# Half-row output stores: the first right-hand tile by itself, two left-hand tiles in one store, and the evictions around them on other engines

## The chip, the cores and the metric

The kernel runs on one core of a Trainium2 chip. The metric is device time in microseconds (us) of one execution, from its start to its end; lower is better.

## The reference

Pooled attention over eight batches and eight heads feeds a soft mixture of experts. What the change touches is the end of the second part.

```python
# attention: k and v are averaged over 8 neighbours, then softmax(q k^T / 8) v
x = attn_out.transpose(0, 2, 1, 3).reshape(4608, 512)     # one row per token
logits = x @ phi                                          # 4608 x 32 slots
d = softmax(logits, axis=0);  slot_input = d.T @ x        # 32 x 512
for e in range(8):                                        # 4 slots for each expert
    slot_out[e] = relu(slot_input[e] @ w1[e]) @ w2[e]     # 512 -> 1024 -> 512
c = softmax(logits, axis=1)
out = c @ slot_out                                        # 4608 x 512, float32
```

## The kernel before, in words

The first 120 us are attention, in four pairs of batches, with the transposed exponentials of the logits left in `cT` (slots on the partitions, tokens in the free dimension). Meanwhile GpSimd's queue loads `w1` and `w2` from memory, converted to bf16 on the way. Then come the hidden layer (`hidden`, `turn_hidden`), the second layer (`second_layer`, L582), which accumulates the 32 slot outputs in the bank `so_ps`, and the combination of the slots into the tokens.

The output is made in 36 tiles of 128 tokens by 512 columns. A group of `rows` tiles holds `128 * rows` neighbouring tokens, partition p having `rows` of them, so that a whole group is stored with long contiguous runs; `GROUPS` and `TILES` say which tile is row r of which group. `tokens(n)` picks the columns of `cT` for tile n, with a step of `rows // 2`.

The columns are cut into a left and a right half of 256. The weights of the last two experts are loaded half by half (L530, in the pieces `PIECES`), first all pieces of the left half, then those of the right. As soon as a half is complete, `begin` makes its first four tiles: `so_a` is the slot outputs without the very last piece of the weights (J7), whose share comes in by a product with `zT` (L659), so that these tiles need not wait for `so`, which is made behind them from the complete `so_ps`. `put` evicts a tile from PSUM and divides it by the token's sum `recR`; its third argument picks the engine, 0 for ScalarE (L616) and 1 for VectorE (L618). `tiles` makes two further tiles of a half (product L639) and stores them. Tiles 0 to 9 are made and stored in halves; the 26 behind them (groups of 4, 8 and 14 rows) in whole rows, with one store for a group.

All stores are issued by SyncE (SP) at L634 in program order, each waiting for the evictions of its tiles. SP does nothing else. The order of instructions on TensorE, ScalarE, VectorE and SP in this part is the order of the code.

The sums over the slots of each token come from products with a one-hot matrix, chunk by chunk (`chunk_sums`, L429): the first three chunks early, the other seven later in two portions. `quads` and `rest` set the order of the chunks; they are built from `GROUPS`.

Of the kernel before, what the change touches and what calls it, by code (L numbers as in the profile page):

```python
# [18 lines left out]
def kernel(  # L19
# [10 lines left out]
    nc = tc.nc  # L30
# [5 lines left out]
    E = moe_w1.shape[0]  # L36
# [12 lines left out]
    FJ = F // 128  # L49
# [4 lines left out]


    GROUPS, base = [], 0
    for rows in (2, 2, 2, 4, 4, 8, 14):
        GROUPS.append((rows, base))
        base += 128 * rows
    TILES = [(g, r) for g, (rows, _) in enumerate(GROUPS) for r in range(rows)]  # L60
# [13 lines left out]
    cT = persist.tile([128, 2, B * S // 2], BF)  # L74
# [89 lines left out]
    with tc.tile_pool(name="tmp", bufs=1) as tmp:  # L164
# [8 lines left out]
        for r in range(2):  # L173
            rows = slice(r * D, (r + 1) * D)
# [11 lines left out]
        for r in range(2):  # L186
            rows = slice(r * D, (r + 1) * D)
# [219 lines left out]
    for g, (rows, base) in enumerate(GROUPS):  # L407
        cols = cT[:, :, base // 2:base // 2 + 64 * rows].rearrange("p r (i s) -> p s r i", s=rows // 2)
# [44 lines left out]
        nc.vector.reciprocal(out=recR[:, 2:4, 0:len(quads)], in_=ps[:, 2:4, 0:len(quads)])  # L453
        yield

    def tokens(n):

        g, r = TILES[n]
        rows, base = GROUPS[g]
        step, c0 = rows // 2, base // 2 + r // 2  # L460
        return cT[:, r % 2, c0:c0 + 127 * step + 1:step]

    def step(gen):
        if gen is not None:
# [52 lines left out]
    def half_home(e, half):  # L517
        if e == E - 1:
            flat = xsa[:, 1, half * FJ * HC:(half + 1) * FJ * HC]
        else:  # L520
            c0 = CUT6 * DM + half * (FJ - CUT6) * HC
            flat = xsa[:, 0, c0:c0 + (FJ - CUT6) * HC]
        return flat.rearrange("p (j c) -> p j c", c=HC)

    w2_half = {}
    for half, cols in enumerate(halves):
        for e, j0, j1 in PIECES:
            home = half_home(e, half)
# [19 lines left out]
    recC = post.tile([128, 1], FP)  # L548
# [25 lines left out]
    so_ps = ps_o.tile([128, DM], FP, name="so_ps")  # L574

    def second_layer(e, j0=0, j1=FJ, half=None, by=1):

        cols = slice(0, DM) if half is None else halves[half]
        for fj in range(j0, j1):
            g = fj % NG  # L580
            rhs = w2_at[e, fj] if half is None else w2_half[e, fj, half]
            nc.tensor.matmul(out=so_ps[g * NS:(g + 1) * NS, cols].rearrange("p (c s) -> p s c", s=by), lhsT=hT[:, e, fj],  # L582
                             rhs=rhs.rearrange("p (c s) -> p s c", s=by),
                             start=(e == 0 and fj < NG), stop=(e == E - 1 and fj >= NG), skip_group_check=True)
# [12 lines left out]
    J7 = FJ - 1  # L597
# [3 lines left out]
    CARRY = 4  # L601
    z_ps = ps_f.tile([128, 2, 128 * CARRY // 2], FP, name="z_ps", tag="f")
    nc.tensor.matmul(out=z_ps, lhsT=hz, rhs=cT[:, :, 0:128 * CARRY // 2], start=True, stop=True)
    zT = post.tile([128, 2, 128 * CARRY // 2], BF)
# [9 lines left out]
    def scaled(engine, dst, src, by):  # L614
        if engine == 0:
            nc.scalar.activation(out=dst, in_=src, func=AF.Copy, scale=by)  # L616
        else:
            nc.vector.tensor_scalar(out=dst, in0=src, scalar1=by, scalar2=None, op0=ALU.mult)  # L618

    so_a = post.tile([128, DM], BF)  # L620
    so = post.tile([128, DM], BF)

    out_a = exf.rearrange("p (n c) -> p n c", c=DM)
    out_b = w1f.rearrange("p (n c) -> p n c", c=DM)
    n = 0
    places = []
    for rows, base in GROUPS:
        home = out_a[:, n:n + rows] if n + rows <= 6 else out_b[:, n - 6:n - 6 + rows]
        places.append((home, out[base:base + 128 * rows].rearrange("(p r) c -> p r c", r=rows)))
        n += rows  # L630

    def store(g, r0, r1, cols):
        home, dst = places[g]
        nc.sync.dma_start(out=dst[:, r0:r1, cols], in_=home[:, r0:r1, cols])  # L634

    def product(n, cols):
        bank = ps_f.tile([128, DM], FP, name="f_ps", tag="f")
        rhs, times = so[:, cols], 2 if cols == halves[0] and n >= CARRY else 1
        nc.tensor.matmul(out=bank[:, 0:times * (cols.stop - cols.start)].rearrange("p (a c) -> p a c", a=times), lhsT=tokens(n),  # L639
                         rhs=rhs.rearrange("p c -> p () c").to_broadcast([128, times, cols.stop - cols.start]),  # L640
                         start=True, stop=True)
        return bank[:, 0:cols.stop - cols.start]

    def rec(n):
        i, c = place[n]
        return recR[:, i, c:c + 1]

    def put(n, cols, engine, ps):
        g, r = TILES[n]
        scaled(engine, places[g][0][:, r, cols], ps, rec(n))  # L650

    def begin(half, stores):

        cols = halves[half]
        scaled(0, so_a[:, cols], so_ps[:, cols], recC)
        f = []
        for n in range(CARRY):
            f.append(ps_f.tile([128, DM], FP, name="f_ps", tag="f")[:, 0:HC])
            nc.tensor.matmul(out=f[n], lhsT=zT[:, n % 2, n // 2 * 128:n // 2 * 128 + 128], rhs=w2_half[E - 1, J7, half],  # L659
                             start=True, stop=False)  # L660
        for n in range(CARRY):
            nc.tensor.matmul(out=f[n], lhsT=tokens(n), rhs=so_a[:, cols], start=False, stop=True)
        second_layer(E - 1, J7, FJ, half)
        put(0, cols, 0, f[0])
        put(1, cols, 1, f[1])
        put(2, cols, 0, f[2])
        scaled(1, so[:, cols], so_ps[:, cols], recC)
        put(3, cols, 0, f[3])
        for g, r0, r1 in stores:
            store(g, r0, r1, cols)  # L670

    def tiles(n0, n1, half):

        cols = halves[half]
        for n in range(n0, n1):
            put(n, cols, 1 - n % 2, product(n, cols))
        g, r = TILES[n0]
        store(g, r, r + n1 - n0, cols)

# [13 lines left out]
    second_layer(*PIECES[1], 0)  # L693
    busy(192)
    second_layer(*PIECES[2], 0)
    begin(0, ((0, 0, 1), (0, 1, 2), (1, 0, 1), (1, 1, 2)))
    for n in (4, 6):
        tiles(n, n + 2, 0)
    for e, j0, j1 in PIECES[:2]:
        second_layer(e, j0, j1, 1)  # L700
    tiles(8, 10, 0)
    for e, j0, j1 in PIECES[2:-1]:
        second_layer(e, j0, j1, 1)
    begin(1, ((0, 0, 2), (1, 0, 2)))
    for n in (4, 6, 8):
        tiles(n, n + 2, 1)
    for n in range(10, len(TILES)):
        g, r = TILES[n]
# [33 lines left out]
```

## Time and profile before

| | us |
|---|---|
| median of 3 runs | 174.5 (174.48 to 174.53) |
| the profiled execution | 174.42 |
| its span, first to last instruction | 172.6 |

| engine | busy us | share of the span |
|---|---|---|
| TensorE | 131.7 | 76% |
| VectorE | 100.8 | 58% |
| ScalarE | 88.0 | 51% |
| GpSimd | 27.5 | 16% |

The 16 transfer engines moved 41.13 MB, at a mean of 238 GB/s. 30.48 MB of it are loads from GpSimd's queue and 10.49 MB transfers from SP's, of which the output is 9.44 MB. The page gives the busy share of the transfer engines as a row of 40 digits, tenths of each slice of the span (4.3 us). The busy shares of the engines are averages over stages with quite different limits, so the tail of the kernel, from about 144 us, has to be read by itself. The times of a store are its issue on SP (start and duration), the first packets, and its landing. A transfer's duration in the table of DMA issues is from issue to landing, and so includes what it waited behind other transfers.

### The profile page before, as it was taken

How to read it: one execution, taken by the hardware profiler on the slowest of the kernel's cores; microseconds unless marked ns; L12 is line 12 of the kernel's file. 1: busy time of each engine (PE TensorE's matmuls, PEld its weight loads, DVE VectorE, ACT ScalarE, POOL GpSimd, SP SyncE). 2: the span in 40 equal slices, each digit the busy share in tenths (PEclk: the TensorE clock that was granted, in tenths of full speed). 3: DMA queues.
4: the chain of work that ended last, by engine and by line, in shares of the span. 5: the costliest groups of instructions: out<-in, count | busy, mean ns of one | idle time of the engine just before them, and what ended most of it. 6: DMA issues, size and time to landing. Idle time of an engine off the chain costs nothing.

```text
span 172.6 us, 2869 instructions
## 1 busy us (share of the span) xinstructions
PE 131.7 (76%) x1106; PEld 71.1 (41%) x1106; DVE 100.8 (58%) x265; ACT 88.0 (51%) x168; POOL 27.5 (16%) x42
## 2 busy tenths in 40 slices
PE   0005798899999999899789999896899997899000
PEld 0002373556555656556345554452452234433000
DVE  6686152569678667887994858841551103599300
ACT  3201336988496846988601998566021003699100
POOL 7000102020201013205100470130610030000000
PEclk9999999999999999999999999999999999999955
DMA  5999999999999999999999999999999999999994
GB/s 196 244 220 222 209 220 218 209 219 218 209 218 217 216 219 214 216 217 211 218 216 215 216 216 220 216 213 216 216 215 216 208 193 195 321 354 425 490 425 213
DMA packets 10589, 41.13 MB, mean 238 GB/s; under 512 B 704, under 2 KB 6592, under 8 KB 6864
## 3 DMA queue, kind: packets, MB, share of 16 engines
q0 software_dynamic: 7248, 30.48, 87.0%
q1 hardware_dynamic: 3328, 10.49, 15.5%
q8 instruction: 8, 0.13, 0.3%
q14 instruction: 5, 0.04, 0.1%
HBM read 61.93 MB, written 9.44 MB: 413 GB/s over the span
## 4 chain that ended last, share of the span: by engine, by line
PE 34%; DMA 27%; ACT 14%; DVE 13%; issue 3%; POOL 1%; DVEq 0%; ACTq 0%; POOLq 0%
DMA xsa<-in_moe_w_dram 21%; PE pool_ps L232 10%; ACT exa L311 7%; DMA phi_f<-in_moe_phi_dram 7%; DVE xsa L342 6%; PE u_ps L331 5%; PE q_ps L264 5%; PE sc L309 5%; PE G_ps L366 3%; PE turn_ps L248 2%; DVE w_sb L618 2%; ACT vmeans L238 2%; PE f_ps L639 2%; ACT vp L296 2%; ACT w_sb L616 1%
## 5 line engine op out<-in xcount | busy, mean ns | idle before, releaser
L311 ACT ACTIVATE exa<-sc 72x576 bf16<-72x576 f32 x64 | 39.3, 653 | 4.6 <-PE sc L309 3.8
L342 DVE TENSOR_TENSOR xsa<-u_ps,rec 128x384 bf16<-128x384 f32 x69 | 37.8, 554 | 1.7
L331 PE MATMUL u_ps<-vp,exa 128*128 128x97 bf16 (+5 forms) x320 | 31.4, 229 | 3.6 <-DVE xsa L342 3.0
L331 PEld LDWEIGHTS <-exa 128*128 128x128 bf16 (+1 forms) x320 | 18.9, 100 | 15.7 <-DVE xsa L342 6.4
L309 PE MATMUL sc<-qTa,kp 64*72 64x288 bf16 x128 | 20.6, 303 | 1.7 <-ACT exa L311 1.2
L232 PE MATMUL pool_ps<-big,pmat 128*128 128x512 bf16 x64 | 18.2, 410 | 0.7 <-ACT qTa L268 0.7
L336 DVE RECIPROCAL rec<-u_ps 128x4 f32<-128x4 f32 x72 | 11.9, 174 | 10.8 <-PE u_ps L331 10.5
L268 ACT COPY qTa<-q_ps 128x768 bf16<-128x768 bf16 x8 | 6.4, 794 | 13.1 <-PE q_ps L264 13.1
L184 PE MATMUL phi_ps<-spread,sel 128*128 128x256 bf16 x4 | 1.3, 395 | 15.0 <-DVE spread L179 15.0
L264 PE MATMUL q_ps<-ident,big 128*128 128x128 bf16 x144 | 12.4, 230 | 0.2
L639 PE MATMUL f_ps<-so,cT 128*128 128x512 bf16 (+1 forms) x38 | 10.1, 361 | 2.0 <-DVE so L618 1.3
L240 DVE TENSOR_REDUCE rsum<-rest_ps 128x64 f32<-128x512 f32 x8 | 5.5, 691 | 10.1 <-PE rest_ps L236 10.1
L309 PEld LDWEIGHTS <-kp 64*72 64x72 bf16 x128 | 7.8, 107 | 8.9 <-issue 3.5
L618 DVE TENSOR_SCALAR w_sb<-f_ps,recR 128x512 f32<-128x512 f32 (+1 forms) x17 | 10.5, 679 | 0.6 <-PE f_ps L639 0.5
L264 PEld LDWEIGHTS <-big 128*128 128x128 bf16 x144 | 9.6, 103 | 2.5 <-issue 1.0
L270 DVE COPY qTa<-q_ps 128x768 bf16<-128x768 bf16 x16 | 8.7, 551 | 2.6 <-PE q_ps L264 2.6
L616 ACT ACTIVATE w_sb<-f_ps,recR 128x512 f32<-128x512 f32 (+1 forms) x17 | 9.5, 637 | 0.7 <-PE f_ps L639 0.5
L530 POOL DMA_DIRECT2D xsa<-in_moe_w_dram x8 | 5.9, 743 | 22.3 <-DMA qTa<-in_moe_w_dram 8.9
L366 PE MATMUL G_ps<-xsa,ee 128*128 128x512 bf16 x36 | 8.4, 379 | 1.2 <-ACT ee L361 1.2
L232 PEld LDWEIGHTS <-pmat 128*128 128x128 bf16 x64 | 6.0, 102 | 6.9 <-issue 2.4
L238 ACT CAST vmeans<-pool_ps 128x1024 bf16<-128x1024 f32 x4 | 4.0, 1012 | 6.8 <-PE pool_ps L232 6.8
L616 ACT ACTIVATE so_a<-so_ps,recC 128x256 bf16<-128x256 f32 x2 | 0.9, 470 | 12.4 <-PE so_ps L582 12.4
(109 smaller groups left out, 168.8 us busy)
## 6 DMA issues: line engine op xcount, KB each, us to landing
w_sb<-in_moe_w_dram POOLq DMA_DIRECT2D x2, 3072.0 KB, 36.7
big<-in_q_dram POOLq DMA_DIRECT2D x4, 1152.0 KB, 12.5
big<-in_v_dram POOLq DMA_DIRECT2D x4, 1152.0 KB, 15.8
big<-in_moe_w_dram POOLq DMA_DIRECT2D x1, 4096.0 KB, 33.3
out_dram<-w_sb SPq DMA_DIRECT2D x1, 3584.0 KB, 10.6
big<-in_k_dram POOLq DMA_DIRECT2D x3, 1152.0 KB, 21.3
w_sb<-in_moe_w_dram POOLq DMA_DIRECT2D x2, 1024.0 KB, 18.3
qTa<-in_moe_w_dram POOLq DMA_DIRECT2D x1, 2048.0 KB, 30.1
```

The source lines that it names most:

```text
L232: nc.tensor.matmul(out=ps, lhsT=pmat, rhs=src[:, t:full * POOL:POOL, :], start=(t == 0), stop=(t == POOL - 1))
L264: nc.tensor.transpose(out=ps[:, t].rearrange("p n i -> p (n i)"), in_=q_sb[pair][:, tt:tt + 2, :].rearrange("p t d -> p (t d)"), identity= ...
L270: nc.vector.tensor_copy(out=dst, in_=ps)
L309: nc.tensor.matmul(out=ps[:, r, 0:S // 2], lhsT=kp[pair][rows, n], rhs=qT[pair][rows, n].rearrange("p t i -> p (t i)"), start=True, stop=True)
L311: nc.scalar.activation(out=dst.rearrange("p r (i t) -> p r i t", t=NU), in_=ps[:, :, 0:S // 2].rearrange("p r (t i) -> p r i t", i=NI), fu ...
L331: nc.tensor.matmul(out=bank[rows, hh * UW:(hh + times) * UW].rearrange("p (a c) -> p a c", a=times), lhsT=ex[b][:, hh].rearrange("p r t -> ...
L336: nc.vector.reciprocal(out=rec, in_=ps[:, :, XW])
L342: nc.vector.tensor_tensor(out=dst, in0=ps[:, :, 0:XW], in1=rec.rearrange("p h -> p h ()").to_broadcast([128, HQ, XW]), op=ALU.mult)
L366: nc.tensor.matmul(out=ps, lhsT=ee[:, t].rearrange("p g s -> p (g s)"), rhs=x[:, t, :, 0:D], start=(t == 0), stop=(t == 8))
L616: nc.scalar.activation(out=dst, in_=src, func=AF.Copy, scale=by)
L618: nc.vector.tensor_scalar(out=dst, in0=src, scalar1=by, scalar2=None, op0=ALU.mult)
L639: nc.tensor.matmul(out=bank[:, 0:times * (cols.stop - cols.start)].rearrange("p (a c) -> p a c", a=times), lhsT=tokens(n), rhs=rhs.rearran ...
```

## The change

There are four edits.

1. The groups of the tiles that are made in halves are of 4 and 6 rows, where they were of 2, 2, 2 and 4; the groups of 4, 8 and 14 rows behind them stay. Tiles keep their numbers, but hold other tokens.
2. The right half stores tile 0 by itself, then tiles 1 and 2, then tile 3; before, it stored tiles 0 and 1, then 2 and 3.
3. The left half stores tiles 0 and 1 by themselves as before, and tiles 2 and 3 in one store instead of two.
4. In the left half, tiles 0, 1 and 2 go to ScalarE and tile 3 to VectorE, with `so` ahead of all of VectorE's evictions; the piece of the second layer that `so` needs stands behind the first of the four products instead of the last. In `tiles`, the even tile of the left half goes to ScalarE and the odd one to VectorE, the other way round from before. In the right half the order and the engines stay.

The core of the diff:

```diff
-    for rows in (2, 2, 2, 4, 4, 8, 14):
+    for rows in (4, 6, 4, 8, 14):
...
         for n in range(CARRY):
             nc.tensor.matmul(out=f[n], lhsT=tokens(n), rhs=so_a[:, cols], start=False, stop=True)
-        second_layer(E - 1, J7, FJ, half)
+            if n == (0 if half == 0 else CARRY - 1):
+                second_layer(E - 1, J7, FJ, half)
         put(0, cols, 0, f[0])
-        put(1, cols, 1, f[1])
-        put(2, cols, 0, f[2])
-        scaled(1, so[:, cols], so_ps[:, cols], recC)
-        put(3, cols, 0, f[3])
-        for g, r0, r1 in stores:
-            store(g, r0, r1, cols)
+        if half == 0:
+            scaled(1, so[:, cols], so_ps[:, cols], recC)
+            put(1, cols, 0, f[1])
+            put(2, cols, 0, f[2])
+            put(3, cols, 1, f[3])
+        else:
+            put(1, cols, 1, f[1])
+            put(2, cols, 0, f[2])
+            scaled(1, so[:, cols], so_ps[:, cols], recC)
+            put(3, cols, 0, f[3])
+        for r0, r1 in stores:
+            store(0, r0, r1, cols)
...
-            put(n, cols, 1 - n % 2, product(n, cols))
+            put(n, cols, (n + half) % 2, product(n, cols))
...
-    begin(0, ((0, 0, 1), (0, 1, 2), (1, 0, 1), (1, 1, 2)))
+    begin(0, ((0, 1), (1, 2), (2, 4)))
...
-    begin(1, ((0, 0, 2), (1, 0, 2)))
+    begin(1, ((0, 1), (1, 3), (3, 4)))
```

Beside these, `of_tile` is `tokens` for any tensor of that layout, used for `zT` as well, and the tiles' homes in the chip's memory are cut at tile 4 instead of tile 6.

SP's stores in order, before. The rows are line, operation, out<-in and shape: `128x256` is one tile's half, `256x1x256` and `128x2x256` are two; `exa` and `w_sb` are the homes of the evicted tiles. The left half ends with the first row of `w_sb`, and the last three rows are whole rows.

```order
L634 DMA out_dram<-exa 128x256 x4
L634 DMA out_dram<-exa 256x1x256
L634 DMA out_dram<-w_sb 128x2x256 x2
L634 DMA out_dram<-exa 256x1x256 x3
L634 DMA out_dram<-w_sb 128x2x256 x2
L634 DMA out_dram<-w_sb 128x2048
L634 DMA out_dram<-w_sb 128x4096
L634 DMA out_dram<-w_sb 128x7168
```

And the same stores of the change:

```order
L637 DMA out_dram<-exa 128x256 x2
L637 DMA out_dram<-exa 128x2x256
L637 DMA out_dram<-w_sb 128x2x256 x3
L637 DMA out_dram<-exa 128x256
L637 DMA out_dram<-exa 128x2x256
L637 DMA out_dram<-exa 128x256
L637 DMA out_dram<-w_sb 128x2x256 x3
L637 DMA out_dram<-w_sb 128x2048
L637 DMA out_dram<-w_sb 128x4096
L637 DMA out_dram<-w_sb 128x7168
```

The left half has six stores instead of seven, the right half six instead of five.

VectorE in both halves of the combination, from the sums' reciprocals on, before (`so` is the slot outputs, the other outs are tiles):

```order
L453 RECIPROCAL recR<-RT_ps 128x2x8
L618 TENSOR_SCALAR exa<-f_ps,recR 128x256
L618 TENSOR_SCALAR so<-so_ps,recC 128x256
L618 TENSOR_SCALAR exa<-f_ps,recR 128x256
L618 TENSOR_SCALAR w_sb<-f_ps,recR 128x256 x2
```

And with the change:

```order
L453 RECIPROCAL recR<-RT_ps 128x2x8
L621 TENSOR_SCALAR so<-so_ps,recC 128x256
L621 TENSOR_SCALAR exa<-f_ps,recR 128x256
L621 TENSOR_SCALAR w_sb<-f_ps,recR 128x256 x3
L621 TENSOR_SCALAR exa<-f_ps,recR 128x256
```

In the left half `so` is now VectorE's first instruction and tile 3 its second; three tiles (5, 7 and 9) follow; the last row is tile 1 of the right half.

More of the change, by code (lines that the diff above doesn't have):

```diff
@@ L454, in slot_sums, with of_tile @@
         yield
-    def tokens(n):
+    def of_tile(t, n):
         g, r = TILES[n]
@@ L460, in tokens @@
         step, c0 = rows // 2, base // 2 + r // 2
-        return cT[:, r % 2, c0:c0 + 127 * step + 1:step]
+        return t[:, r % 2, c0:c0 + 127 * step + 1:step]
+    def tokens(n):
+        return of_tile(cT, n)
     def step(gen):
@@ L627 @@
     for rows, base in GROUPS:
-        home = out_a[:, n:n + rows] if n + rows <= 6 else out_b[:, n - 6:n - 6 + rows]
+        home = out_a[:, n:n + rows] if n + rows <= 4 else out_b[:, n - 4:n - 4 + rows]
         places.append((home, out[base:base + 128 * rows].rearrange("(p r) c -> p r c", r=rows)))
@@ L658, in begin @@
             f.append(ps_f.tile([128, DM], FP, name="f_ps", tag="f")[:, 0:HC])
-            nc.tensor.matmul(out=f[n], lhsT=zT[:, n % 2, n // 2 * 128:n // 2 * 128 + 128], rhs=w2_half[E - 1, J7, half],
+            nc.tensor.matmul(out=f[n], lhsT=of_tile(zT, n), rhs=w2_half[E - 1, J7, half],
                              start=True, stop=False)
```

## The prediction

> **What bounds the kernel now.** I read the page first, for the transfers.
>
> ```profile
> span 172.6 us, 2869 instructions
> DMA  5999999999999999999999999999999999999994
> out_dram<-w_sb SPq DMA_DIRECT2D x1, 3584.0 KB, 10.6
> ```
>
> The profiled run took 174.42 us, 1.8 us more than its span of 172.6 us. The transfer engines are at 9 tenths or more in every slice but the first and the last. The stores of the output are all that is left behind the last of the weights, and the last store (3584 KB) needs 10.6 us from issue to landing. So I asked next for the busy time by stage of the tail. The last three columns are the granted clock, the DMA share and GB/s.
>
> ```profile
> 144.00:146.50 2.50, 1.78 (x13) 1.15 (x13) 0.96 (x2) 1.68 (x4) 0.00 (x0) 1.00 1.45 196
> 146.50:148.00 1.50, 1.50 (x15) 0.52 (x13) 0.91 (x2) 0.91 (x2) 0.00 (x0) 1.00 1.35 244
> 148.00:148.50 0.50, 0.45 (x5) 0.19 (x3) 0.35 (x1) 0.13 (x1) 0.00 (x0) 1.00 1.06 333
> 148.50:149.00 0.50, 0.43 (x6) 0.24 (x4) 0.13 (x1) 0.50 (x2) 0.00 (x0) 1.00 0.87 301
> 149.00:151.00 2.00, 1.35 (x12) 0.90 (x10) 0.97 (x2) 1.41 (x4) 0.00 (x0) 1.00 1.06 365
> 151.00:151.50 0.50, 0.42 (x4) 0.22 (x3) 0.48 (x2) 0.37 (x1) 0.00 (x0) 1.00 0.73 248
> 151.50:155.00 3.50, 3.24 (x13) 1.38 (x13) 3.35 (x7) 3.50 (x8) 0.00 (x0) 1.00 1.04 346
> 155.00:163.00 8.00, 4.51 (x16) 1.76 (x14) 6.08 (x10) 5.07 (x9) 0.00 (x0) 1.00 1.11 462
> 163.00:171.00 8.00, 0.00 (x0) 0.00 (x0) 0.00 (x0) 0.00 (x0) 0.00 (x0) 0.57 0.93 401
> ```
>
> Up to 146.5 us only weights move (196 GB/s as written to the chip), then weights and stores together, from 148.5 us only stores: 365 GB/s for half rows, 401 to 462 for whole ones. There are two dips. From 148.5 to 149.0 the rate is 301 instead of 365: 0.5 x (1 - 301/365) = 0.09 us lost, and with the half microsecond ahead of it (333: 0.04 us, some of it still weights) 0.13 us. From 151.0 to 151.5 it is 248: 0.5 x (1 - 248/365) = 0.16 us lost. Behind them no stretch has a hole. The tail is transfer work with 0.29 us of idle in it; what the change can win is there.
>
> The chain of waits tells what starts the right half:
>
> ```profile
> 140.51 8.18 DMA xsa<-in_moe_w_dram
> 148.74 0.61 PE f_ps L659 x4
> ```
>
> It is the landing of the last weights at 140.51 + 8.18 = 148.69 us. Last, the timeline of SP's queue, one store each (start, duration of the issue):
>
> ```profile
> 145.68 0.34 SPq L634 DMA_DIRECT2D out_dram<-exa  x1
> 147.04 0.45 SPq L634 DMA_DIRECT2D out_dram<-exa  x1
> 147.59 0.62 SPq L634 DMA_DIRECT2D out_dram<-exa  x1
> 148.94 0.45 SPq L634 DMA_DIRECT2D out_dram<-w_sb  x1
> 150.23 0.55 SPq L634 DMA_DIRECT2D out_dram<-exa  x1
> 151.63 0.53 SPq L634 DMA_DIRECT2D out_dram<-exa  x1
> 153.91 0.34 SPq L634 DMA_DIRECT2D out_dram<-w_sb  x1
> 161.16 0.33 SPq L634 DMA_DIRECT2D out_dram<-w_sb  x1
> ```
>
> These are the first, fourth, fifth and last (seventh) store of the left half, the first and third of the right half, and the first and last of whole rows. On the left SP issues without a pause, 0.34 to 0.62 us each. When do packets follow? The second dip ends here:
>
> ```profile
> 151.40:151.50 0.10, 0.02 (x1) 0.00 (x0) 0.10 (x2) 0.10 (x1) 0.00 (x0) 1.00 0.74 256
> 151.50:151.60 0.10, 0.04 (x1) 0.04 (x1) 0.10 (x2) 0.10 (x2) 0.00 (x0) 1.00 1.02 348
> ```
>
> The store issued from 150.23 to 150.78 us brings the rate back at about 151.48: packets run 0.7 us behind the end of the issue. The first dip ends likewise at 147.59 + 0.62 + 0.7 = 148.91, when the fifth left store arrives. Both dips are waits for a store that SP issued late.
>
> **The change, part by part.**
>
> *Left half, order and engines.* Now ScalarE evicts tiles 0, 1 and 2, and VectorE makes `so` first and tile 3 behind it.
>
> ```profile
> 145.18 1.20 ACT L616 ACTIVATE exa<-f_ps,recR 128x256 f32<-128x256 f32 x3 [0.36 <-PE f_ps L662]
> 145.29 0.48 DVE L618 TENSOR_SCALAR exa<-f_ps,recR 128x256 f32<-128x256 f32 x1 [2.41 <-PE f_ps L662]
> 145.80 0.48 DVE L618 TENSOR_SCALAR so<-so_ps,recC 128x256 bf16<-128x256 f32 x1
> ```
>
> VectorE's first eviction (0.48 us) no longer stands ahead of `so`, so `so` ends at about 145.8 instead of 145.80 + 0.48 = 146.28, and the products of tiles 4 to 7 come 0.5 us earlier. ScalarE has three evictions in 1.20 us as before, so tile 2 is ready at 146.38; tile 3 is ready by 146.3 on VectorE.
>
> *Left half, stores.* Six issues instead of seven. The first two start where they did; the third, with tiles 2 and 3, at 146.55, its inputs being ready by then. At 0.55 us for a 256 KB issue and 0.08 us between issues it ends at 147.15, and the store of tiles 4 and 5 at about 147.75 instead of 148.21: its packets come at 148.45, 0.46 us earlier than 148.91, just about where the first dip begins. I take 0.10 of its 0.13 us as won. Tiles 8 and 9 still wait for weights, and for them SP has time.
>
> *Does this push the weights back?* The third store carries 256 KB from 147.85 us (147.15 + 0.7) where two of 128 KB came at 147.69 and 148.19 (fourth issue: 147.04 + 0.45 + 0.7). In the row of 146.5 to 148.0 the mean is 244 GB/s, so weights still fill most of it, and by 148 us they are nearly done: I take nothing, at most 0.1 us either way.
>
> *Right half, first store.* Tile 0 goes alone. Its eviction and the chain behind it on ScalarE and VectorE stay:
>
> ```profile
> 149.56 1.20 ACT L616 ACTIVATE exa<-f_ps,recR 128x256 f32<-128x256 f32 x3 [0.36 <-PE f_ps L662]
> 149.67 0.48 DVE L618 TENSOR_SCALAR exa<-f_ps,recR 128x256 f32<-128x256 f32 x1 [1.04 <-PE f_ps L662]
> 151.42 0.48 DVE L618 TENSOR_SCALAR w_sb<-f_ps,recR 128x256 f32<-128x256 f32 x1
> 151.50 0.47 ACT L616 ACTIVATE w_sb<-f_ps,recR 128x256 f32<-128x256 f32 x1
> ```
>
> Tile 0 is ready at 149.56 + 0.47 = 150.03 (one eviction by the last row), tile 1 at 149.67 + 0.48 = 150.15. The first issue, after a wait, takes 0.34 us by the first left one: 150.06 to 150.40, packets at 151.10 instead of 151.48. That closes the second dip: 0.16 us.
>
> *Right half, the stores behind it.* Three issues stand now where two stood. Tiles 1 and 2 (ready at 150.4): 150.46 to 150.96 at 0.5 us, packets at 151.66. Tile 3: 151.03 to 151.48, packets at 152.18. Tiles 4 and 5: before, their issue starts at 151.63, and it waits for their evictions, which this change leaves where they are. So it starts at 151.63 again, packets at 151.63 + 0.53 + 0.7 = 152.86. Now the transfer engines' side: 128 KB takes 131,072 / 365 GB/s = 0.36 us, 256 KB 0.72 us. Left stores end at about 151.2; tile 0 lasts to 151.56; a hole of 0.10; tiles 1 and 2 to 152.38; tile 3 to 152.74; a hole of 0.12 until 152.86. Before, two stores of 0.72 us from 151.48 ended at 152.92, hardly later than those packets came. So almost all that is won ahead is lost again at this store, whose issue nothing moves: the gain is 152.92 - 152.86 = 0.06 us, up to 0.13 if that old store was waiting somewhat longer. Behind it everything is bound as before.
>
> A rule speaks against this part. A 128 KB store is issued in no less time than it moves: 0.45 us of SP for 0.36 us of transfer. The Trainium skill (DMA: Bandwidth & Descriptors, section Anatomy of one DMA) gives each DMA a fixed cost of about 2.0 us beside its bytes; charged to the right half's one more store, that would be an estimated 2 us. The four small left stores here contradict a charge in series:
>
> ```profile
> out_dram<-exa SPq DMA_DIRECT2D x4, 128.0 KB, 3.3
> ```
>
> They land 3.3 us behind their issue, but four of them are issued within 145.68 to 147.49. The fixed time lies beside other packets wherever the queue isn't empty.
>
> *Row groups and sums.* Tiles 0 to 9 now come in groups of four and six rows, so the kernel reads tokens with a step of 2 or 3 instead of 1 or 2, and the sums for the rows swap chunks: the chunk of tiles 0 to 3 goes ahead into the three early ones, that of tiles 14 to 17 behind.
>
> ```profile
> 117.24 1.06 PE L429 MATMUL R_ps<-cT,onehot 128*10 128x512 bf16 x3
> 128.83 2.19 PE L429 MATMUL R_ps<-cT,onehot 128*10 128x512 bf16 x3
> 134.68 1.69 PE L429 MATMUL R_ps<-cT,onehot 128*10 128x512 bf16 x4
> 144.02 0.29 PE L582 MATMUL so_ps<-xsa,hT 128*32 128x256 bf16 x3 [0.15 <-DMA xsa<-in_moe_w_dram]
> ```
>
> Early chunks mean 1.06 / 3 = 0.35 us, late ones (2.19 + 1.69) / 7 = 0.55. A chunk of a wider step takes the place of a narrow one, so TensorE is 0.2 to 0.3 us later in the 130s. The waits for weights hide it, of which the last is 0.15 us at 144.02. Without that cover the left half starts 0.1 us later, and it has more than that in hand before its stores are missed. I take nothing. Bytes, 1 KB pieces and the count of stores (fifteen) stay.
>
> **The sum.** 174.42 - 0.06 = 174.36, as 174.4 us; the profiled run stands 0.08 us under the median of 174.5, which is inside what I can claim. A run of this kernel tells from no change about 0.2%, or 0.35 us, so I forecast no change.
>
> **The rivals.**
>
> *Slower, SP is the bound of the right half.* If the first three right issues, 1.42 us in my sum, take 0.62 us each (the longest row) with 0.08 between them, they end at 150.06 + 3 x 0.70 = 152.16, and tiles 4 and 5 go out 0.53 us late. Minus the 0.1 us in hand that is 0.43 us: 174.85. It decides once the three take over 1.57 + 0.1 us. For it: the 0.62 row came right behind four small stores. Against: an issue after a wait took 0.34 us. 0.20.
>
> *The earlier left stores delay the last weights.* Then right tile 0, and tiles 4 and 5, move back with them, by 0.1 to 0.2 us: 174.5 to 174.6, no change. Against it: most weights are in by 148 us. 0.14.
>
> *Faster, both dips go and the right half then runs at the left half's rate.* 0.29 us, and 3.5 x (1 - 346/365) = 0.18 us: 173.95. It needs the stores of tiles 4 and 5 out sooner, which nothing in the diff does, unless weights land sooner. 0.14.
>
> *Each store's fixed time counts in series.* One more small store on an empty queue would add, by its row above, 3.3 - 0.4 = 2.9 us: 177.3. Against it stand the four stores that overlap. 0.02. (This is the Trainium skill's fixed cost per DMA, from the section named above, taken without overlap.)
>
> **Numbers.** My forecast has 0.50 (174.3 to 174.42), with the late weights 0.64 for no change; faster 0.14; slower 0.22. The range 174.0 to 174.9 holds the first three cases and the near edge of the faster one.
>
> **What would show it.** Right steps: a left store of tiles 4 and 5 issued by 147.3; DMA share 1.0 or more through 148.5 to 149.0; the first right issue at 150.06 and the fourth at 151.63; the last store landing within 0.15 us of 171.76 (161.16 + 10.6 before). I am wrong if the fourth right issue is 0.2 us or more off 151.63, if the last weights land 0.2 us or more off 148.69, or if the rate from 151.5 to 155 us rises to 365.

## The result, and the profile after

The change is 0.2% faster: 174.13 us (174.0 to 174.26, 14 runs) against 174.48 us (174.41 to 174.75, 14 runs), a ratio of 0.9978 with a 95% interval of 0.9971 to 0.9985. Measured again beside other kernels it gave 0.9983 (0.9974 to 0.9992). The profiled run took 174.13 us, with a span of 172.3 us.

The tail of the changed kernel by stage, columns as before (the last three are granted clock, DMA share, GB/s):

```profile
148.00:148.50 0.50, 0.36 (x5) 0.18 (x3) 0.18 (x1) 0.40 (x1) 0.00 (x0) 1.00 1.13 357
148.50:149.00 0.50, 0.45 (x6) 0.23 (x6) 0.30 (x1) 0.32 (x2) 0.00 (x0) 1.00 1.09 383
149.00:151.00 2.00, 1.35 (x12) 0.93 (x10) 0.97 (x2) 1.42 (x4) 0.00 (x0) 1.00 1.03 357
151.00:151.50 0.50, 0.44 (x5) 0.26 (x3) 0.46 (x2) 0.35 (x1) 0.00 (x0) 1.00 0.99 336
151.50:155.00 3.50, 3.22 (x13) 1.35 (x13) 3.36 (x7) 3.50 (x8) 0.00 (x0) 1.00 1.08 371
163.00:171.00 8.00, 0.00 (x0) 0.00 (x0) 0.00 (x0) 0.00 (x0) 0.00 (x0) 0.50 0.93 401
...
152.50:153.00 0.50, 0.50 (x4) 0.21 (x3) 0.50 (x1) 0.50 (x2) 0.00 (x0) 1.00 1.06 359
...
150.60:151.00 0.40, 0.27 (x3) 0.26 (x3) 0.08 (x1) 0.18 (x1) 0.00 (x0) 1.00 0.86 300
```

The first dip is gone (383 GB/s where 301 stood). The second has moved ahead and shrunk, but it isn't closed: 300 GB/s from 150.6 to 151.0 us, and 336 in the half microsecond behind it, where 248 stood. The stretch from 151.5 to 155 us runs at 371 instead of 346 GB/s. In its middle, from 152.5 to 153.0, where I expected a hole ahead of tiles 4 and 5, there is none.

SP's queue: the first, third and fourth left store, the six of the right half, and the last of all.

```profile
145.72 0.34 SPq L637 DMA_DIRECT2D out_dram<-exa  x1
146.63 0.40 SPq L637 DMA_DIRECT2D out_dram<-exa  x1
147.22 0.38 SPq L637 DMA_DIRECT2D out_dram<-w_sb  x1
150.08 0.34 SPq L637 DMA_DIRECT2D out_dram<-exa  x1
150.52 0.39 SPq L637 DMA_DIRECT2D out_dram<-exa  x1
151.00 0.44 SPq L637 DMA_DIRECT2D out_dram<-exa  x1
151.65 0.37 SPq L637 DMA_DIRECT2D out_dram<-w_sb  x1
152.12 0.44 SPq L637 DMA_DIRECT2D out_dram<-w_sb  x1
152.66 0.44 SPq L637 DMA_DIRECT2D out_dram<-w_sb  x1
161.18 0.33 SPq L637 DMA_DIRECT2D out_dram<-w_sb  x1
```

The starts are where they were forecast (150.06 and 151.63), but look at the durations. Every store of two tiles now takes 0.37 to 0.45 us to issue; before, the right one of tiles 4 and 5 took 0.53 us and the fifth left one 0.62.

```profile
140.53 8.18 DMA xsa<-in_moe_w_dram
...
out_dram<-w_sb SPq DMA_DIRECT2D x1, 3584.0 KB, 10.2
```

By the chain of waits the weights land at 140.53 + 8.18 = 148.71 us, 0.02 us later than before. By the table of DMA issues the last store takes 10.2 us from its issue at 161.18, so it lands at about 171.4 us; before, the same sum gave 171.76, and the trace has 171.72. That is 0.3 us, as much as the span became shorter.

### The profile page after: what moved, and what is told of

Same layout as the page of the kernel before. It is cut to its first block, busy times and chain, and to the rows that moved or that the text cites. A ratio compares the mean times of both kernels' runs of the same rounds, so it can differ in the third digit from the quotient of the medians.

```text
span 172.3 us, 2868 instructions
## 1 busy us (share of the span) xinstructions
PE 131.0 (76%) x1106; PEld 70.1 (41%) x1106; DVE 100.6 (58%) x265; ACT 88.1 (51%) x168; POOL 27.5 (16%) x42
## 4 chain that ended last, share of the span: by engine, by line
PE 33%; DMA 28%; DVE 15%; ACT 12%; issue 3%; POOL 1%; DVEq 0%; POOLq 0%; ACTq 0%
DMA xsa<-in_moe_w_dram 21%; PE pool_ps L232 10%; DMA phi_f<-in_moe_phi_dram 7%; ACT exa L311 7%; DVE xsa L342 6%; PE u_ps L331 5%; PE sc L309 5%; PE q_ps L264 4%; DVE w_sb L621 4%; PE G_ps L366 3%; PE turn_ps L248 2%; ACT vmeans L238 2%; DVE rsum L240 2%; ACT vp L296 2%; DVE rec L336 2%
## 5 line engine op out<-in xcount | busy, mean ns | idle before, releaser
L621 DVE TENSOR_SCALAR w_sb<-f_ps,recR 128x512 f32<-128x512 f32 (+1 forms) x19 | 11.3, 660 | 1.5 <-DMA xsa<-in_moe_w_dram 0.7
L264 PE MATMUL q_ps<-ident,big 128*128 128x128 bf16 x144 | 11.6, 219 | 0.8 <-DVE qTa L270 0.3
L619 ACT ACTIVATE w_sb<-f_ps,recR 128x512 f32<-128x512 f32 (+1 forms) x19 | 10.3, 620 | 1.3 <-PE f_ps L642 1.1
L264 PEld LDWEIGHTS <-big 128*128 128x128 bf16 x144 | 8.7, 97 | 3.0 <-issue 1.4
## 6 DMA issues: line engine op xcount, KB each, us to landing
out_dram<-w_sb SPq DMA_DIRECT2D x1, 3584.0 KB, 10.2
```

The source lines that it names most:

```text
L264: nc.tensor.transpose(out=ps[:, t].rearrange("p n i -> p (n i)"), in_=q_sb[pair][:, tt:tt + 2, :].rearrange("p t d -> p (t d)"), identity= ...
```

## The experiments

Three parts can be told apart: the row groups (edit 1), the right half's order of stores (edit 2), and the left half (edits 3 and 4). Two theories stood at first. By A the order of the stores fills the holes. By B the groups do it: two tiles of a two-row group are stored by SP as `256x1x256`, two of a four- or six-row group as `128x2x256`. The first form is called the old or dear one below, the second the new or cheap one.

**The groups alone.**

```diff
-            if n == (0 if half == 0 else CARRY - 1):
-                second_layer(E - 1, J7, FJ, half)
+        second_layer(E - 1, J7, FJ, half)
...                                    # evictions and engines as before the change
-    begin(0, ((0, 1), (1, 2), (2, 4)))
+    begin(0, ((0, 1), (1, 2), (2, 3), (3, 4)))
-    begin(1, ((0, 1), (1, 3), (3, 4)))
+    begin(1, ((0, 2), (2, 4)))
```

> Only the row groups of the change (4 and 6 rows); order of evictions, engines and stores as before. Theory A (the gain is filled holes, by the order of stores): no gain, 174.4 to 174.5, holes of 0.1 us at 148.5 to 149.0 and 0.16 us at 151.0 to 151.5 as before. Theory B (the groups do it: a store of two tiles is now 128x2x256 on SP, cheaper to issue than 256x1x256, and its packets run faster): at least half of the 0.35 us, 174.3 or less; the two-tile issues take 0.37 to 0.45 us instead of 0.53 to 0.62, and the rate from 151.5 to 155 us rises from 346 to about 370 GB/s.

It took 174.25 us, a ratio of 0.9983 (0.9974 to 0.9992) to the kernel before (174.53 in these runs): 0.28 us, most of the gain, without any new order. Its first and third right store, and two stretches of its tail:

```profile
150.30 0.37 SPq L637 DMA_DIRECT2D out_dram<-exa  x1
151.70 0.37 SPq L637 DMA_DIRECT2D out_dram<-w_sb  x1
...
148.50:149.00 0.50, 0.44 (x5) 0.24 (x5) 0.21 (x1) 0.50 (x2) 0.00 (x0) 1.00 1.03 352
151.00:151.50 0.50, 0.49 (x5) 0.31 (x4) 0.40 (x2) 0.30 (x1) 0.00 (x0) 1.00 0.88 307
```

The two-tile issues take 0.37 us where 0.55 and 0.53 stood, and both dips are shallower (352 and 307 GB/s against 301 and 248), with the orders of before. That is B's side, though the rate behind 151.5 us rose only to 352, not to the 370 it named.

**The left half alone, on the old groups.**

```diff
+        if half == 0:
+            scaled(1, so[:, cols], so_ps[:, cols], recC)
+            put(1, cols, 0, f[1])
...
-    begin(0, ((0, 0, 1), (0, 1, 2), (1, 0, 1), (1, 1, 2)))
+    begin(0, ((0, 0, 1), (0, 1, 2), (1, 0, 2)))
```

> The old row groups, with the left half of the change: so ahead on VectorE, engines swapped, tiles 2 and 3 in one store. Theory A: the hole at 148.5 to 149.0 closes (share above 1.0), 0.1 us faster at the half stores, 174.4 at the end. Theory B: nothing, or slower, because three stores of the dear form follow one another on SP; 174.45 to 174.6.

174.57 us, ratio 1.0 (0.9991 to 1.0009). Nothing, as B had it; 0.06 us against it comes from the count of stores, below.

**The change with the old right half, and with the old left half.**

```diff
-    begin(1, ((0, 1), (1, 3), (3, 4)))
+    begin(1, ((0, 2), (2, 4)))
```

> The changed kernel with the right half's first stores as before: tiles 0 and 1, then 2 and 3. Theory A: the hole at 151 us comes back, at 0.16 us or more since the left stores end sooner; 174.3. Theory B: the first store of two tiles is issued after a wait in 0.37 us, so the hole is 0.1 us smaller than before, and nearly all of the gain stays: 174.15 to 174.2.

174.31 us, ratio 0.9987 (0.9978 to 0.9995). As it stands this is A's number; less the 0.06 us that come from the count of stores, below, it lies between the two theories, and the interval can't tell them apart. The hole is B's: 297 GB/s, where 248 stood before the change.

```profile
151.00:151.50 0.50, 0.50 (x5) 0.40 (x4) 0.31 (x1) 0.20 (x1) 0.00 (x0) 1.00 0.85 297
```

```diff
-    begin(0, ((0, 1), (1, 2), (2, 4)))
+    begin(0, ((0, 1), (1, 2), (2, 3), (3, 4)))
...                                    # evictions and engines of the left half as before
```

> The changed kernel with the left half as before (so behind tile 1, old engines, four stores of one tile). Theory A: the hole at 148.5 to 149.0 comes back, 0.1 us slower than the change: 174.25. Theory B: as the change, 174.1 to 174.2.

174.57 us, ratio 1.0001 (0.9992 to 1.001). This fits neither theory: the whole gain is gone, although its last store lands when that of the change does. What differed was the end: its span ran on for longer behind that landing. This kernel issues sixteen stores, the change fifteen. So a third theory, C: the end depends on which landing signal the last store uses. D, its rival: the early left order was worth it.

> The changed kernel with the left half's tiles 2 and 3 in two stores again, all else as changed: sixteen stores instead of fifteen. Theory C (the stores use eight landing signals in turn, and SP checks them at the end in a fixed order, 0.06 us each; with fifteen stores the last one's signal is the last checked, with sixteen seven checks follow its landing): 7 x 0.06 = 0.42 us slower than the change at the same landing of the last store, 174.55. Theory D (the early left order itself was worth the 0.4 us that the kernel with the old left half lost): 174.1 to 174.2, since the order is kept.

The diff is the one line `begin(0, ...)` just shown, with the change's evictions kept.

> The changed kernel, its six left stores kept, with the old evictions in the left half (tile 1 and then so on VectorE, tiles 2 and 3 on ScalarE, old engines for tiles 4 to 9): fifteen stores. Theory C: the evictions are worth nothing by themselves, 174.1 to 174.2. Theory D: 0.3 us or more lost, 174.45 or more.

Its diff is the other half: the old evictions, with `begin(0, ((0, 1), (1, 2), (2, 4)))` kept.

Sixteen stores: 174.56 us (1.0006, 0.9997 to 1.0015). Old evictions, fifteen stores: 174.14 us (0.9981, 0.9972 to 0.9989). The difference is 0.42 us, as worked out for C; D falls. The trace shows it. First the changed kernel, then the one with sixteen stores: the last store's issue and time to landing, SP's instructions of the closing line behind 171 us, and the span.

```profile
161.18 0.33 SPq L637 DMA_DIRECT2D out_dram<-w_sb  x1
DMA to landing us min/median/max: 10.2/10.2/10.2
L747 SPq EVENT_SEMAPHORE  x3: 17/17/28, 171.4 to 172.3; - x3
core 0: 172.3 us, clock 0.973
```

```profile
161.20 0.33 SPq L637 DMA_DIRECT2D out_dram<-w_sb  x1
DMA to landing us min/median/max: 10.2/10.2/10.2
L747 SPq EVENT_SEMAPHORE  x10: 17/28/28, 171.5 to 172.7; - x10
core 0: 172.8 us, clock 0.968
```

Both stores land at 171.4 us. Behind it the changed kernel's SP has three semaphore instructions left, the other ten: seven more checks, 0.06 us from one to the next. SP's transfers use eight landing signals in turn, and at the end SP checks all eight in a fixed order: in each trace the transfers carry the numbers 108 and 112 to 118 in turn, and the closing instructions wait for them from 108 to 118. The load at the start and fifteen stores are sixteen transfers, so the last one is on the eighth signal, which is checked last; with one store more it is on the first, and seven checks that could have been made long before stand behind it. With fourteen stores one check does, 0.06 us, which belongs to the two runs above with that count. The changed kernel with the old right half is one of them:

```profile
L747 SPq EVENT_SEMAPHORE  x4: 17/22/28, 171.6 to 172.5; - x4
```

All thirteen traces agree: from the end of the last packet to the end of the span it is 1.32 to 1.33 us with fourteen stores, 1.25 to 1.27 with fifteen and 1.67 with sixteen.

**One pair of the old form.** What do the groups win: SP's time (S), or faster writes because of the layout in memory (L)?

```diff
-    for rows in (4, 6, 4, 8, 14):
+    for rows in (4, 2, 4, 4, 8, 14):
```

> The changed kernel with groups of 4, 2 and 4 rows instead of 4 and 6, so that only the stores of tiles 4 and 5 take the form 256x1x256; order, engines and count of stores as changed. Theory S (what the groups win is SP's time: a 256x1x256 store is issued in 0.53 to 0.62 us instead of 0.37 to 0.45 and the next one is late too): the right store of tiles 4 and 5 is issued in 0.53 us, a small hole or a lower rate follows, 0.05 to 0.15 us of the gain lost, 174.2 to 174.3. Theory L (layout in memory: the groups of four and six rows are written faster): nothing lost beyond 0.03 us.

174.38 us, ratio 0.9993 (0.9984 to 1.0002), 0.24 us slower than the old-evictions kernel beside it (174.14). The right stores of tiles 4 and 5, then of tiles 6 and 7, and two stretches:

```profile
151.62 0.55 SPq L637 DMA_DIRECT2D out_dram<-w_sb  x1
152.27 0.55 SPq L637 DMA_DIRECT2D out_dram<-w_sb  x1
...
152.50:153.00 0.50, 0.50 (x4) 0.20 (x3) 0.50 (x1) 0.50 (x2) 0.00 (x0) 1.00 0.81 277
```

The start is unmoved, the issue takes 0.55 us instead of 0.37, the next one, though of the cheap form, takes 0.55 too instead of 0.44, and a hole opens just where such a store's packets are due, at 277 GB/s against the change's 359. The direction is S's. The loss is larger than I had put it by the medians; the profiled run took 174.28 us, 0.15 us more than that of the old-evictions kernel (174.13).

**The new orders on the old groups.**

```diff
-    begin(1, ((0, 0, 2), (1, 0, 2)))
+    begin(1, ((0, 0, 1), (0, 1, 2), (1, 0, 2)))
...                                    # left half as changed
```

> The old groups of two rows with the orders of the change: left half as changed, right half with tile 0, then tile 1, then tiles 2 and 3; fifteen stores. Theory S: the holes ahead of tiles 4 and 5 are won and lost again at the dear issue of that store, 0 to 0.1 us faster than before, 174.4 to 174.5. Theory A (order alone fills the holes): 0.25 us faster, 174.25.

174.50 us, ratio 1.0001 (0.9992 to 1.0011). A's 174.25 is out. The right half's third store and five stretches:

```profile
151.06 0.55 SPq L634 DMA_DIRECT2D out_dram<-exa  x1
...
148.50:149.00 0.50, 0.44 (x5) 0.24 (x5) 0.33 (x1) 0.31 (x2) 0.00 (x0) 1.00 1.08 367
149.00:151.00 2.00, 1.35 (x12) 0.91 (x11) 0.97 (x2) 1.46 (x4) 0.00 (x0) 1.00 1.06 365
...
149.10:149.80 0.70, 0.70 (x7) 0.43 (x5) 0.07 (x1) 0.34 (x2) 0.00 (x0) 1.00 1.06 364
149.80:150.50 0.70, 0.32 (x3) 0.19 (x2) 0.68 (x2) 0.70 (x3) 0.00 (x0) 1.00 1.07 372
...
151.90:152.30 0.40, 0.40 (x3) 0.10 (x2) 0.40 (x2) 0.40 (x3) 0.00 (x0) 1.00 0.41 141
```

The first dip is closed here as well. Then the two single tiles are soon through, and the dear store behind them, issued to 151.61, brings packets at 152.3: until then the rate is 141 GB/s. What the order wins ahead is lost at that store. The rows of 149.1 to 150.5 us speak against L. Counted by packets, the left store of tiles 4 and 5, of the form `256x1x256`, passes from 149.12 to 149.84 us, and that of tiles 6 and 7, of the other form, from there to 150.55: 364 and 372 GB/s with a full queue. The 2% between them are 0.015 us for a store, far from 0.24. Their packets aren't slow; they come late.

**The same pair behind a longer queue** (groups of 4, 2 and 4 rows, right stores in pairs).

> The groups of 4, 2 and 4 rows with the right half's first stores in pairs (tiles 0 and 1, then 2 and 3), so that half a megabyte is queued when the right store of tiles 4 and 5, of the form 256x1x256, is issued in 0.53 to 0.55 us. Fourteen stores, so it stands against the changed kernel with the old right stores (174.31, ratio 0.9987). Theory S (SP's issue time, which counts where little is queued): the same within 0.05 us, no hole behind 152.5 us. Theory L (the packets of that form are slower): 0.2 us slower, 174.5, as with the single pair group and the new right stores.

174.49 us, ratio 1.0001 (0.9988 to 1.0014): S's expectation failed, and the time is the one that L named. The queue wasn't long enough.

```profile
150.50 0.37 SPq L637 DMA_DIRECT2D out_dram<-exa  x1
151.90 0.55 SPq L637 DMA_DIRECT2D out_dram<-w_sb  x1
...
152.80:153.20 0.40, 0.40 (x3) 0.14 (x2) 0.40 (x1) 0.40 (x2) 0.00 (x0) 1.00 0.66 223
```

Two pairs, due from 150.50 + 0.37 + 0.7 = 151.57, last 1.44 us, to 153.0; the dear store is due at 151.90 + 0.55 + 0.7 = 153.15. The hole is there (223 GB/s). As a time, this run doesn't tell S from L; that the engines stood idle at that place again is S's mark, and the rates of the two forms above are what rules L out. Keeping the groups and changing only the form of a store was not tried.

**An attempt at a better version**: tiles 0 and 1 of the left half in one store, 2 and 3 alone.

```diff
-    begin(0, ((0, 1), (1, 2), (2, 4)))
+    begin(0, ((0, 2), (2, 3), (3, 4)))
```

> The changed kernel with the left half's tiles 0 and 1 in the first store and tiles 2 and 3 in a store each, fifteen stores again. The first packets come 0.4 us later, so the last weights should land up to 0.1 us sooner, and the hole of 0.08 us at 150.7 us in the changed kernel shrink. If holes and landing are all: 174.05 to 174.1. If weights and stores share the engines without loss either way: 174.13.

> The changed kernel itself, on the same chip as the two runs beside it, for the comparison: ratio 0.998, 174.1 to 174.2.

174.18 us (0.9979, 0.997 to 0.9987) against 174.19 us for the change beside it (0.9983, 0.9974 to 0.9992). No difference. That weights and stores share the engines without loss isn't shown by it, for the hole did shrink (348 GB/s from 150.6 to 151.0 us, where the change has 300), and the time didn't follow. The right store of tiles 4 and 5 is issued as late as ever:

```profile
150.60:151.00 0.40, 0.23 (x3) 0.22 (x3) 0.12 (x1) 0.22 (x1) 0.00 (x0) 1.00 1.01 348
...
151.69 0.37 SPq L637 DMA_DIRECT2D out_dram<-w_sb  x1
```

No kernel tried beats the change.

## Why the prediction was right or wrong

The forecast was no change beyond 0.2%, at 174.4 us; measured is 0.22% faster, at 174.13, inside the range. So the time was held, and the gain undersized: 0.06 us forecast against 0.35. That the time fell inside is owed to the width of the range (0.9 us) and not to the sum: 174.13 lies below the 174.3 to 174.42 of the forecast itself, at the near edge of the faster rival.

Of the prediction's own signs, the issue of the left store of tiles 4 and 5 (147.22 us), the DMA share of the first dip (1.09), the first and the fourth right issue (150.08 and 151.65) and the weights (148.71) came as named. Two went against it: the last store landed more than 0.3 us ahead of 171.76, and the rate from 151.5 to 155 us rose to 371 GB/s, which it had named as a sign of being wrong.

- *The tail is transfer work with holes in it, and the gain is bounded by what the holes hold.* Right. Holes and the rate between 151.5 and 155 us (346 to 371 GB/s) are the change.
- *First dip*: the sum took 0.10 of its 0.13 us as won, and it closed. Of the reasons given, one store fewer and an earlier `so`, the second wasn't needed: with the old evictions the left store of tiles 4 and 5 starts at 147.49 us instead of 147.22, and the rate from 148.5 to 149.0 is 371 GB/s all the same. (A small slip: 146.55 + 0.55 is 147.10, not 147.15.)
- *Second dip*: the sum took all of its 0.16 us as won by the first right tile alone. About 0.11 is left: 0.4 x (1 - 300/365) = 0.07 and 0.5 x (1 - 336/365) = 0.04, the latter with the hole that was forecast ahead of tiles 1 and 2 in it. The left stores end sooner, so the hole opens sooner.
- *The hole ahead of tiles 4 and 5*: the wrong step. The sum issued the right store of tiles 4 and 5 in 0.53 us, the row of the old form, and concluded that nothing moves its packets. It starts at 151.65 as forecast but takes 0.37 us, so its packets are due at 151.65 + 0.37 + 0.7 = 152.72 and find the engines still at work. With 0.55 us the forecast was a good one: the kernel with one pair of the old form, which has the change's orders, took 174.38 us, where the sum gave 174.36.
- *What this step decides.* Counted by packets, the first packet of this store starts at 152.99 us before and at 152.74 with the change, where the sum had 152.92 and 152.86. So 0.06 us became 0.25: 0.07 because the old store did wait for the queue, as the prediction allowed for, and 0.12 by the shorter issue. In all thirteen traces the last packet of the run ends 18.31 to 18.38 us behind this one, whatever stands ahead of it (171.37 before, 171.07 with the change). A hole that is filled ahead of this store is worth only what it moves this store's first packet.
- *Row groups: taken as nothing.* That is the same miss. I priced them on TensorE and in memory, not on SP, though the order of SP's stores showed the new form. Alone they gave 0.28 us.
- *Left evictions, TensorE's sums, weights*: no effect on the time. The weights landed 0.02 us later; old evictions gave 174.14.
- *The rivals.* SP as the bound decides, but the other way: the issues became shorter, not longer, and the first three right ones ended at 151.44 us, against 151.48 in the sum. The faster rival named the thin supply between 151.5 and 155 us, and that is where a part came from; it asked for the stores of tiles 4 and 5 to be out sooner, and missed that a shorter issue does that. A fixed time in series did not show. (The section of the Trainium skill that the prediction names for it, Anatomy of one DMA in DMA: Bandwidth & Descriptors, is about transfers that GpSimd issues; these stores are SP's.)
- *The count of stores* I took as a mere sum of work that stays. That it stays at fifteen was worth 0.42 us: the right half's additional store needs the left half's merged one. Without the merge the change would have been no gain (1.0006). The prediction didn't look behind the last landing, so it is luck that this term was nothing here.

How much the new orders add to the groups isn't settled: 174.13 and 174.19 against 174.25 us, with intervals of about 0.15 us each way.

## What to carry to other kernels

When a stage is bound by transfers that one queue issues, price each issue by its shape, and see whether the next packets arrive before the last ones are through: one issue that took 0.18 us longer, with 0.11 on the next, cost 0.24 us at the end, by the medians, where nothing was queued. Ask of a layout change what it does to the descriptors' shape and not only to the engines that read the data. And when two versions differ in the count of transfers, look at what the program does behind the last landing before explaining their times by what lies ahead of it.

## What the runs showed of the hardware

- A store of two half tiles takes SP 0.53 to 0.62 us to issue as 256 rows of 256 elements, and 0.37 to 0.45 us as 128 x 2 x 256, for the same bytes in the same 1 KB pieces; one issued right behind the dear form is slower too (0.53 to 0.56 us). Once queued, the two forms move alike (364 and 372 GB/s).
- Packets start about 0.7 us behind the end of an issue, in every hole that was looked at.
- SP's closing checks of landing signals take 0.06 us each, in a fixed order, so the last transfer's place among eight decides up to 0.42 us of a 174 us kernel (14, 15 and 16 stores were run).
